# Two fused attention-and-FFN layers on one core: PSUM banks of phase A, one staged weight, reloads and low parts put in other places

## The chip, the cores and the metric

The kernel runs on one core of a Trainium2 chip. Its engines work side by side: TensorE (PE) multiplies matrices into eight PSUM banks, VectorE (DVE), ScalarE (ACT) and GpSimd (POOL) do the elementwise work, and SyncE (SP) issues most of the DMAs. The metric is the device time of one execution in microseconds, the median over several runs. The times of the profile are microseconds from the start of the profiled span unless they are marked ns.

## The reference

Two layers, with the same weights in both, run over x of 2048 rows and 640 columns:

```python
x = x + A(layernorm(x), wqkv, wo)
x = x + B(layernorm(x), w1, b1, w2, b2)      # and both once more
# A, 32 heads of 20: phi(t) = where(t > 0, t + 1, exp(t)) + 1e-6
kv  = einsum("bhsd,bhse->bhde", phi(k), v);  z = einsum("bhsd->bhd", phi(k))
o   = einsum("bhqd,bhde->bhqe", phi(q), kv) / (einsum("bhqd,bhd->bhq", phi(q), z)[..., None] + 1e-6)
A   = o @ wo
# B: h = x @ w1 + b1 (640 -> 1728);  B = max(h, 0)**2 @ w2 + b2 (1728 -> 640)
```

All of it is in float32.

## The kernel before

**Split numbers.** Each float32 matrix is held as a high part (rounded to the fast matmul type) and a low part (the rest). A product is three matmuls: low of one by high of the other, the other way round, and high by high. The high part is made by ACT (a copy), the low part by DVE (a subtraction), so the low part is always the later one.

**Phase A** (`for t in range(NT)`) goes through 16 tiles of 128 rows. For each tile it multiplies the normalised, transposed x (`xT`) by the weights of k and q (`kq`, five chunks, 1280 KB each with both parts), makes phi from the PSUM result (ACT takes the exponential, DVE the rest), and adds to G = xᵀ·phi(k) in banks 3 to 7 (`g_part`) for the tile before. The last 128 columns of k go to GT (`gt_part`), once for each pair of tiles; DVE adds that PSUM result to `GT_` (L613). Banks 0, 1 and 2 (`XB`) are for the parts of k and q and for GT. Tiles named in `LATE` compute only k in the loop ("late" tiles); their q follows afterwards. In such a tile the first part goes to bank 0, the second to bank 1, GT to banks 2 and 0; the next tile's first part goes to bank 0 again. In layer 0 ACT also moves blocks for the transpose of x (L459, sixteen moves for a tile), and `Prep` cuts w1 and w2 into high and low parts between the tiles: `prep_step(t, i)` is called at four places of each tile and takes one staged piece at each of them (`low`, then `high`; the high part is an ACT copy of what a DMA has brought, L295).

**Between the phases** kv is made from G, multiplied into wo, and split (`m_split`, L1050 the high part, L1051 the low part) into the five chunks of M. `proj` multiplies the first four tiles by M, and DVE adds the result to x, normalises it (`b_x1`, L748, L363, L373) and splits it for FC1 (L121).

**Phase B** runs in four groups of four tiles (512 rows). FC1 has 14 steps (`fc1`, 15 matmuls of 512 columns for most), FC2 has 28 steps (`fc2_step`, 7 products of 4 units each, in the order `ORDER`). The weights come from DRAM: `Units` holds a ring of six buffers, refilled in the order of use each time one comes free (`load_ring`, L338). Unit 0 of each of the seven products is loaded once for each layer and stays in the "w" buffers. Those five buffers hold, at other times, the five chunks of `kq`. Everything else is hung on steps: `at(g, n, f)` runs f after step n of group g (steps from NF = 14 on are those of FC2). `single` prepares the tiles of the next group: x goes out to DRAM (`spread_out`, issued by POOL), comes back in another order (`spread_in`, four DMAs issued by SP, L410), DVE transposes it (`turn`, L420), and ACT and DVE split it. `ffn_events` splits the hidden values into units of a small arena (ACT L1229, DVE L1233). The rows of ones and zeros that carry b2 are written by POOL memsets (L1157, L1158 at the start, L1161, L1162 in `ones_row`). `side_last` runs in the last group of layer 0: it reloads `kq` for layer 1 (L201) and prepares layer 1's first three tiles.

Instructions run in program order on each engine; SP's DMAs are issued in program order as well, and one that must wait for its buffer holds up those behind it. A new tile of a pool takes a buffer whose last use lies earlier in the program.

Of the kernel before, what the change touches and what calls it, by code (L numbers as in the profile page):

```python
# [17 lines left out]
DC = D // P  # L18
# [47 lines left out]
def kernel(  # L66
# [25 lines left out]
    def bank(i, n=1):  # L92
        return PS[:, 512 * i : 512 * (i + n)]
# [57 lines left out]
    class FirstLoads:  # L151


        def __init__(self):
            self.todo = [(nm, c) for nm in ("k", "q") for c in range(DC)]
            self.pending = []

            self.halves = []
# [160 lines left out]
    class Units:  # L319


        def __init__(self):
            self.at = {}
            self.ring = list(uses)
            self.stay = [(m, 0) for m in ORDER]
            self.spare = []
            self.free = 0
# [21 lines left out]
                self.at[m, k] = u  # L349

        def used(self, g, nm, c):
            if nm == "w1" or c > 0:
                self.free += 1

        def get(self, g, nm, c):
            return self.at[(nm, c) if nm != "w1" and c == 0 else (g, nm, c)]

    sts = {}

# [135 lines left out]
    def proj(ps, aT, w, cs=range(DC)):  # L495

        for c in cs:
            for j in range(2):
                s = slice(j * HD, (j + 1) * HD)
                mm3(  # L500
                    ps[:, j * 512 : j * 512 + HD], aT[:, 0, c, :], aT[:, 1, c, :],
                    w[c][:, 0, s], w[c][:, 1, s], c == 0, c == DC - 1,
                )

    x2 = [dram.tile([P, D], F32, name=f"x2_{t}", tag=f"x2_{t}") for t in range(NT)]

# [25 lines left out]
    for layer in range(N_LAYERS):  # L532
# [151 lines left out]

        pq, xr, pT, yzp, yzx, xn = {}, {}, {}, {}, {}, {}
        dens, xTb = {}, {}
        wu = Units()

        def b_load_pq(t):
            if t < NT:  # L690
# [102 lines left out]
        def prep_step(t, i):  # L793
            if layer == 0 and t in PREP_AT:
                if i == 0:
                    prep.mix()
                    prep.load(PREP.get(t + 1, ""))
                prep.low()
                prep.high()
                if i % 2 == 0:  # L800
                    prep.store(2)

        late = LATE[layer]
        q_end = None
        for t in range(NT):
            first = t == 0 and layer == 0
            early = t == 0 and layer > 0
# [64 lines left out]
            is_late = t in late  # L872
            f, fq = Phi(rtile()), None if is_late else Phi(ftile("rq"))
            n0 = HD if is_late else 512
            ps = ps_first if layer == 0 and t == 1 else part(t, 0, n0, bank(XB[0]))
            gs(0 if is_late or t == 1 and layer == 0 else 2)
            move(t + 1)
            f.exp(0, ps)
# [9 lines left out]
                x_begin(t + 2)  # L888
            f.rest()
            gt = t % 2 == 0 and t > 0  # L890
            ps = part(t, n0, D if is_late else 1024, bank(XB[1]))
            x_low = []
            if t + 1 in yza:
                x_low.append(xT_split(t + 1, x_end(t + 1), True))
# [16 lines left out]
                out=xh[t][:, 1], in0=xt[t], in1=xh[t][:, 0].bitcast(F32), op=ALU.subtract  # L911
            )
            if gt and not is_late:
                gt_part(t // 2 - 1, 0, bank(XB[0]))
            gs(1)
            prep_step(t, 2)
            if is_late:
                gs(1)
                if gt:
                    gt_part(t // 2 - 1, 0, bank(XB[2]))  # L920
                gs(1)
                if gt:
                    gt_part(t // 2 - 1, 1, bank(XB[0]))
            else:
                ps = part(t, 1024, 2 * D, bank(XB[2]))
                gs(1)
            k_post(t, f.r, [lambda: a_stats(t + 3)])
            if gt and not is_late:
                gt_part(t // 2 - 1, 1, bank(XB[1]))
            prep_step(t, 3)  # L930
            gs(DC)
            if not is_late:

                def q_end(t=t, f=fq, ps=ps):
                    f.exp(1024 - D, ps)
                    f.rest()
                    nc.sync.dma_start(pqd[t], f.r)

            move(t + 2, AHEAD)
        if q_end:  # L940
            q_end()
# [212 lines left out]
        )  # L1154

        R = bp.tile([P, 2, 2, KH, HT], F32, name="R", tag="R", bufs=1)
        nc.gpsimd.memset(R[FL:, :, 1, KH - 1], 0.0)  # L1157
        nc.gpsimd.memset(R[FL : FL + 1, :, 1, KH - 1], 1.0)  # L1158

        def ones_row():  # L1160
            nc.gpsimd.memset(R[FL:, 0, 1, KH - 1], 0.0)  # L1161
            nc.gpsimd.memset(R[FL : FL + 1, 0, 1, KH - 1], 1.0)  # L1162

        x1_odd["tile"] = bp.tile([P, TG, D], F32, name="x1", tag="x1", bufs=1)
        arena = tmp.tile([P, SLOTS, 2, 2, HT], R32, tag="T", name="arena", bufs=2)
# [2 lines left out]
        def fc1(g, c):  # L1168
            ps = bank(c % 4)
            u = wu.get(g, "w1", c)  # L1170
            xhi, xlo = xTb[0][:, 0], xTb[0][:, 1]
            if c == 13:
                w = u.rearrange("p (d f) -> p d f", d=DC)
                seq = [(w, xlo), (w, xhi)]
            else:
                w, wl = (u[:, j * D : (j + 1) * D].rearrange("p (d f) -> p d f", d=DC) for j in range(2))
                seq = [(w, xlo), (wl, xhi), (w, xhi)]
            for d in range(DC):
                for i, (a, bb) in enumerate(seq):
                    nc.tensor.matmul(  # L1180
                        ps, a[:, d, :], bb[:, d, :],
                        start=d == 0 and i == 0, stop=d == DC - 1 and i == len(seq) - 1,
                    )
            wu.used(g, "w1", c)
            return ps

# [105 lines left out]
        def at(g, n, f):  # L1292
            events.setdefault((g, n), []).append(f)
# [19 lines left out]
        def single(g, i):  # L1313

            t, b = TG * (g + 1) + i, OUTS[i]

            def on(n, f):
                if n < 0 and g > 0:
                    at(g - 1, NF + N_STEPS + 2 * n, f)
                elif n >= NF:  # L1320
                    at(g, NF + int(2 * (n - NF)), f)
                else:
                    at(g, max(n, 0), f)

# [12 lines left out]
            def out():  # L1337
                yzp.pop(t)
                for j in range(2):
                    s = slice(j * HD, (j + 1) * HD)  # L1340
                    ps.append(bank(6 + j)[:, :HD])
                    for c in range(DC):
                        a = pT[t][:, :, c * P : (c + 1) * P]
                        mm3(ps[j], a[:, 0], a[:, 1], M[c][:, 0, s], M[c][:, 1, s], c == 0, c == DC - 1)
                pT.pop(t)

            def add():
                for j in range(2):
# [12 lines left out]

            def load():
                yzx[t] = spread_in(xd.pop(t))

            n = NF + (1, 5, 9, 13)[i]
            at(g, n, load)
            steps(lambda: x_split(t), (g, n + 4), (g, n + 5), (g, n + 6))

        def ffn_events(g):
            for k in range(PAIRS):  # L1370
                at(g, 6 + k, lambda k=k: u_hi(g, k))
                at(g, 7 + k, lambda k=k: u_lo(g, k))
            for k in range(3):
                at(g, 9 + 2 * k, lambda k=k: s_op(1, k))
            at(g, 11, lambda: u_hi(g, PAIRS))
            at(g, 12, lambda: u_lo(g, PAIRS))
            s = NF
            if g > 0:
                at(g, 1, ones_row)
            at(g, s, lambda: s_op(1, 3))  # L1380
            for n in range(PAIRS + 1, N_STEPS):
                at(g, s + n - 4, lambda n=n: u_hi(g, n))
                at(g, s + n - 3, lambda n=n: u_lo(g, n))
            for k in range(PAIRS):
# [25 lines left out]
        def side_last():  # L1410
# [1 line left out]
                return  # L1412
            g, s = NG - 1, NF
            at(g, 2, lambda: load_kq(0))
            for c, n in ((1, 5), (2, 13), (3, 21), (4, 25)):
                at(g, s + n, lambda c=c: load_kq(c))
            xs = {}

# [6 lines left out]
            for t in range(3):  # L1425
                at(g, 1 + t, lambda t=t: a_load(t, x2))
                at(g, 4 + t, lambda t=t: a_stats(t))
                at(g, 5 + t, lambda t=t: a_apply(t))
                at(g, 6 + t, lambda t=t: store(t))
                at(g, s + 2 + 3 * t, lambda t=t: load(t))  # L1430
            for t in range(2):
                at(g, s + 8 + 4 * t, lambda t=t: xT_split(t, turn(yz0[t], True)))

# [66 lines left out]
```

## Time and profile before

| | before |
|---|---|
| median of the runs | 1346.39 us |
| lowest run | 1344.09 us |
| the profiled execution's own time | 1345.85 us |
| its span in the profile | 1344.1 us |
| mean granted PE clock | 0.997 |
| HBM read and written | 241.51 MB and 65.54 MB |

The page gives for each engine how long it was busy in the span. The waits name, for each line, what ended the idle time ahead of its instructions. In a timeline each row has the start, the duration, the engine, the line, what is written and read, the count, and in brackets the idle time before it with its releaser. In a table of stretches the columns are, after the stretch: its length, the busy time of PE, of PE's weight loads, of DVE, ACT and POOL (each with its count), the granted clock of PE, the mean share of the 16 DMA engines, and GB/s.

### The profile page before, as it was taken

What the parts mean: (1) busy time and instruction counts of PE and PEld (TensorE: products, weight loads), DVE (VectorE), ACT (ScalarE), POOL (GpSimd) and SP (SyncE); (2) the same over time, 40 slices, a digit from 0 to 9 for tenths busy, and PEclk for the clock granted to TensorE, in tenths of its full rate; (3) what the DMA queues carried; (4) which work ended last, traced back from release to release, by engine and by line L of the source; (5) the groups of instructions that cost most, each with busy time, mean ns of one, the idle gap of its engine ahead of it and who ended that gap; (6) DMA issues with size and microseconds to landing.
All of it is one profiled execution on the core that took longest, in us unless ns stands there. A gap on an engine that the chain in (4) does not pass through costs nothing.

```text
span 1344.1 us, 20919 instructions
## 1 busy us (share of the span) xinstructions
PE 1323.4 (98%) x7525; PEld 1202.6 (89%) x7525; DVE 848.4 (63%) x1575; ACT 733.0 (55%) x1594; POOL 166.7 (12%) x259
## 2 busy tenths in 40 slices
PE   8999999999999999999999999999999999999999
PEld 7888898989989988998978889888899899889888
DVE  7888957756844854833746677576567558458045
ACT  4888957785375457334313233387743753754342
POOL 2324310121001001001012222101100010010000
PEclk9999999999999999999999999999999999999999
DMA  6798993489974985896954456454869649749756
GB/s 196 219 282 268 337 343 120 153 327 373 320 296 146 291 306 169 265 359 222 346 185 128 128 133 172 118 192 151 304 207 319 248 161 317 305 148 297 277 190 215
DMA packets 134607, 320.28 MB, mean 238 GB/s; under 512 B 16663, under 2 KB 61847, under 8 KB 133864
## 3 DMA queue, kind: packets, MB, share of 16 engines
q1 hardware_dynamic: 127272, 296.65, 65.0%
q0 software_dynamic: 7232, 22.29, 6.4%
q8 instruction: 60, 0.98, 0.3%
q14 instruction: 43, 0.35, 0.1%
HBM read 241.51 MB, written 65.54 MB: 228 GB/s over the span
## 4 chain that ended last, share of the span: by engine, by line
PE 81%; DVE 6%; DMA 5%; ACT 5%; issue 2%; POOL 0%; SPq 0%; DVEq 0%; ACTq 0%; POOLq 0%
PE PS L473 29%; PE PS L1180 28%; PE PS L1249 22%; DMA z<-xb 3%; ACT z L459 2%; PE PS L1022 1%; DMA u<-kept 1%; DMA kq<-kept_kq 1%; DVE bn L363 1%; ACT z L439 1%; DMA xb<-xt 1%; DVE xT L489 0%; PE PS L831 0%; DVE y L420 0%; PE PS L621 0%
## 5 line engine op out<-in xcount | busy, mean ns | idle before, releaser
L1180 PE MATMUL PS<-xTb,u 128*128 128x512 f32 x1640 | 376.8, 390 | 1.0 <-DVE xTb L121 1.0
L1180 PEld LDWEIGHTS PS<-xTb,u 128*128 128x128 f32 x1640 | 306.7, 188 | 64.1 <-DVE xTb L121 1.5
L473 PE MATMUL PS<-kq,xT 128*128 128x320 f32 (+2 forms) x1575 | 286.0, 335 | 7.4 <-DVE GT L613 3.8
L473 PEld LDWEIGHTS PS<-kq,xT 128*128 128x128 f32 x1575 | 251.4, 189 | 36.1 <-issue 4.9
L1249 PE MATMUL PS<-u,arena 128*128 128x320 f32 x1680 | 257.5, 310 | 3.8 <-DMA u<-kept 2.4
L1249 PEld LDWEIGHTS PS<-u,arena 128*128 128x128 f32 x1680 | 248.8, 188 | 5.7 <-DVE arena L1233 2.7
L1233 DVE TENSOR_TENSOR arena<-R,arena 128x512 fp32r<-128x512 f32 x224 | 136.7, 616 | 137.9 <-ACT arena L1229 137.4
L1229 ACT ACTIVATE arena<-R 128x512 fp32r<-128x512 f32 x224 | 125.1, 572 | 142.3 <-PE PS L1249 136.9
L439 ACT ACTIVATE z<-y 32x160 f32<-32x160 f32 x512 | 171.2, 334 | 50.7 <-DVE y L430 43.2
L1192 ACT ACTIVATE R<-PS,b1sb 128x512 f32<-128x512 f32 x104 | 71.5, 688 | 131.4 <-PE PS L1180 130.4
L473 PE MATMUL PS<-kh,xh 128*128 128x512 f32 x480 | 126.2, 397 | 2.8 <-DVE xT L489 2.4
L473 PE MATMUL PS<-uM,pTs 128*128 128x320 f32 x720 | 109.4, 309 | 0.0
L473 PEld LDWEIGHTS PS<-uM,pTs 128*128 128x128 f32 x720 | 107.4, 188 | 1.9
L1249 PE MATMUL PS<-uw,arena 128*128 128x320 f32 x672 | 107.8, 309 | 0.0
L473 PEld LDWEIGHTS PS<-kh,xh 128*128 128x128 f32 x480 | 88.3, 190 | 18.8 <-DVE xT L489 2.6
L367 POOL TENSOR_SCALAR rs<-mv 128x1 f32<-128x1 f32 x64 | 35.0, 547 | 540.0 <-DVE mv L365 540.0
L1249 PEld LDWEIGHTS PS<-uw,arena 128*128 128x128 f32 x672 | 101.0, 188 | 0.2
L1210 DVE TENSOR_TENSOR R<-R 128x512 f32<-128x512 f32 (+1 forms) x128 | 78.3, 616 | 27.7 <-ACT R L1193 27.7
L459 ACT ACTIVATE z<-y 32x160 f32<-32x160 f32 x272 | 90.9, 334 | 4.5 <-DVE y L430 1.4
L575 ACT ACTIVATE r<-PS 128x512 f32<-128x512 f32 (+1 forms) x64 | 27.7, 434 | 105.5 <-PE PS L473 103.4
L582 DVE TENSOR_SCALAR r<-r 128x512 f32<-128x512 f32 (+1 forms) x64 | 21.1, 329 | 76.2 <-ACT r L575 76.0
L1193 ACT ACTIVATE R<-R 128x512 f32<-128x512 f32 x104 | 65.8, 633 | 3.3
(131 smaller groups left out, 1244.2 us busy)
## 6 DMA issues: line engine op xcount, KB each, us to landing
u<-kept SPq DMA_DIRECT2D x112, 640.0 KB, 5.9
u<-kept_w SPq DMA_DIRECT2D x104, 640.0 KB, 5.0
u<-kept SPq DMA_DIRECT2D x56, 320.0 KB, 6.1
kept<-uprep SPq DMA_DIRECT2D x49, 320.0 KB, 5.5
z<-xb SPq DMA_DIRECT2D x160, 80.0 KB, 5.3
pqt<-pq SPq DMA_DIRECT2D x32, 320.0 KB, 4.6
acc<-r POOLq DMA_DIRECT2D x28, 320.0 KB, 4.1
uw<-kept SPq DMA_DIRECT2D x14, 640.0 KB, 9.1
```

Of the source, the lines that this page charges most:

```text
L367: nc.gpsimd.tensor_scalar(rs, mv[:, 1:2], LN_EPS, None, op0=ALU.add)
L439: nc.scalar.activation(zv[j * B32 : (j + 1) * B32, :, i, :], yv[i * B32 : (i + 1) * B32, :, j, :], AF.Copy)
L459: nc.scalar.activation(zv[j * B32 : (j + 1) * B32, :, i, :], yv[i * B32 : (i + 1) * B32, j], AF.Copy)
L473: nc.tensor.matmul(ps, a, b, start=first and i == 0, stop=last and i == 2)
L575: nc.scalar.activation(self.e[:, a:b], ps, AF.Exp)
L1180: nc.tensor.matmul(ps, a[:, d, :], bb[:, d, :], start=d == 0 and i == 0, stop=d == DC - 1 and i == len(seq) - 1,)
L1192: nc.scalar.activation(r, v, AF.Relu, bias=b1sb[:, c : c + 1])
L1193: nc.scalar.activation(r, r, AF.Square)
L1210: nc.vector.tensor_tensor(out=quad(*out, k), in0=quad(*x, k), in1=quad(*y, k), op=op)
L1229: nc.scalar.activation(u[:, 0], v, AF.Copy)
L1233: nc.vector.tensor_tensor(out=u[:, 1], in0=v, in1=u[:, 0].bitcast(F32), op=ALU.subtract)
L1249: nc.tensor.matmul(ps, x, y, start=opens and k == 0 and p == 0 and e == 0, stop=k == PAIRS - 1 and p == b - a - 1 and e == 2, skip_group_c ...
```

## The change

1. **Banks.** `XB` is copied into a list `xb`; after a late tile with a GT part the list is rotated by one, so that the next tile begins in the next bank.
2. **One staged weight.** In layer 0, and in the last group alone, unit 0 of the last product (4) no longer comes from the buffer where it stays: it is one more load of the ring, ahead of unit 1 of that product. Its buffer's last use is then in the group before.
3. **k/q reload and bounced tiles.** With that buffer, chunk 4 of `kq` is reloaded at FC1 step 4 of the last group, not at FC2 step 25. The three bounced tiles of layer 1 come back at FC1 steps 10 to 12, not at FC2 steps 2, 5 and 8. The bounced tiles of `single` come back at FC2 steps 0, 3, 7 and 11, not at 1, 5, 9 and 13.
4. **Low parts last.** `proj` takes, for each chunk, low·high, high·high and then high·low, each for both halves. The first FC1 step of group 0 takes all products with the high part of x first and those with its low part at the end.
5. **One high part later.** `prep_step` leaves out the `high` of its first place in tile 1; the pieces follow one place later.
6. **Rows of ones.** The memset of both halves at the start of phase B is gone; `ones_row` takes a half and runs for the first group after FC1 steps 12 and 13.

```diff
-        def __init__(self):
+        def __init__(self, short):
             self.at = {}
             self.ring = list(uses)
+            self.moved = (NG - 1, ORDER[-1], 0) if short else None
+            if short:
+                self.ring.insert(self.ring.index((NG - 1, ORDER[-1], 1)), self.moved)
...
         def used(self, g, nm, c):
-            if nm == "w1" or c > 0:
+            if nm == "w1" or c > 0 or (g, nm, c) == self.moved:
                 self.free += 1
         def get(self, g, nm, c):
-            return self.at[(nm, c) if nm != "w1" and c == 0 else (g, nm, c)]
+            at_ring = nm == "w1" or c > 0 or (g, nm, c) == self.moved
+            return self.at[(g, nm, c) if at_ring else (nm, c)]
...
         for c in cs:
-            for j in range(2):
-                s = slice(j * HD, (j + 1) * HD)
-                mm3(
-                    ps[:, j * 512 : j * 512 + HD], aT[:, 0, c, :], aT[:, 1, c, :],
-                    w[c][:, 0, s], w[c][:, 1, s], c == 0, c == DC - 1,
-                )
+            for k, l in ((1, 0), (0, 0), (0, 1)):
+                for j in range(2):
+                    nc.tensor.matmul(
+                        ps[:, j * 512 : j * 512 + HD], aT[:, k, c, :], w[c][:, l, j * HD : (j + 1) * HD],
+                        start=c == 0 and (k, l) == (1, 0), stop=c == DC - 1 and (k, l) == (0, 1),
+                    )
...
-        wu = Units()
+        wu = Units(layer < N_LAYERS - 1)
...
                 prep.low()
-                prep.high()
+                if (t, i) != (1, 0):
+                    prep.high()
...
+        xb = list(XB)
...
-            ps = ps_first if layer == 0 and t == 1 else part(t, 0, n0, bank(XB[0]))
+            ps = ps_first if layer == 0 and t == 1 else part(t, 0, n0, bank(xb[0]))
...
+            if gt and is_late:
+                xb.append(xb.pop(0))
             move(t + 2, AHEAD)
...
-        nc.gpsimd.memset(R[FL:, :, 1, KH - 1], 0.0)
-        nc.gpsimd.memset(R[FL : FL + 1, :, 1, KH - 1], 1.0)
-        def ones_row():
-            nc.gpsimd.memset(R[FL:, 0, 1, KH - 1], 0.0)
-            nc.gpsimd.memset(R[FL : FL + 1, 0, 1, KH - 1], 1.0)
+        def ones_row(h):
+            nc.gpsimd.memset(R[FL:, h, 1, KH - 1], 0.0)
+            nc.gpsimd.memset(R[FL : FL + 1, h, 1, KH - 1], 1.0)
...
-            for d in range(DC):
-                for i, (a, bb) in enumerate(seq):
-                    nc.tensor.matmul(
-                        ps, a[:, d, :], bb[:, d, :],
-                        start=d == 0 and i == 0, stop=d == DC - 1 and i == len(seq) - 1,
-                    )
+            order = [(d, i) for d in range(DC) for i in range(len(seq))]
+            if g == 0 and c == 0:
+                order = [(d, i) for d, i in order if i] + [(d, 0) for d in range(DC)]
+            for d, i in order:
+                a, bb = seq[i]
+                nc.tensor.matmul(
+                    ps, a[:, d, :], bb[:, d, :], start=(d, i) == order[0], stop=(d, i) == order[-1],
+                )
...
             n = NF + (1, 5, 9, 13)[i]
-            at(g, n, load)
+            at(g, NF + (0, 3, 7, 11)[i], load)
...
-            if g > 0:
-                at(g, 1, ones_row)
+            for h in range(2 if g == 0 else 1):
+                at(g, 12 + h if g == 0 else 1, lambda h=h: ones_row(h))
...
             at(g, 2, lambda: load_kq(0))
-            for c, n in ((1, 5), (2, 13), (3, 21), (4, 25)):
+            at(g, 4, lambda: load_kq(4))
+            for c, n in ((1, 5), (2, 13), (3, 21)):
                 at(g, s + n, lambda c=c: load_kq(c))
...
-                at(g, s + 2 + 3 * t, lambda t=t: load(t))
+                at(g, 10 + t, lambda t=t: load(t))
```

In the rest of the tile loop every `XB[...]` becomes `xb[...]`.

More of the change, by code (lines that the diff above doesn't have):

```diff
@@ L890 @@
             gt = t % 2 == 0 and t > 0
-            ps = part(t, n0, D if is_late else 1024, bank(XB[1]))
+            ps = part(t, n0, D if is_late else 1024, bank(xb[1]))
             x_low = []
@@ L913 @@
             if gt and not is_late:
-                gt_part(t // 2 - 1, 0, bank(XB[0]))
+                gt_part(t // 2 - 1, 0, bank(xb[0]))
             gs(1)
@@ L919 @@
                 if gt:
-                    gt_part(t // 2 - 1, 0, bank(XB[2]))
+                    gt_part(t // 2 - 1, 0, bank(xb[2]))
                 gs(1)
                 if gt:
-                    gt_part(t // 2 - 1, 1, bank(XB[0]))
+                    gt_part(t // 2 - 1, 1, bank(xb[0]))
             else:
-                ps = part(t, 1024, 2 * D, bank(XB[2]))
+                ps = part(t, 1024, 2 * D, bank(xb[2]))
                 gs(1)
@@ L928 @@
             if gt and not is_late:
-                gt_part(t // 2 - 1, 1, bank(XB[1]))
+                gt_part(t // 2 - 1, 1, bank(xb[1]))
             prep_step(t, 3)
```

## The prediction

> **What bounds the kernel now.** First the page: the span, and each engine's share.
>
> ```profile
> span 1344.1 us, 20919 instructions
> PE 1323.4 (98%) x7525; PEld 1202.6 (89%) x7525; DVE 848.4 (63%) x1575; ACT 733.0 (55%) x1594; POOL 166.7 (12%) x259
> ```
>
> PE sets the time: it is idle for only 1344.1 - 1323.4 = 20.7 us, and no matmul is removed or added. Whatever the change gives must come out of these 20.7 us, or out of matmuls that run slowly; 2% of the time is 27 us. So the second view is that of PE's waits.
>
> ```profile
> PE PS L473 <- DVE GT L613: 3.8, 2, 2.6
> PE PS L473 <- DMA kq<-kept_kq: 2.8, 1, 2.8
> PE PS L1249 <- DMA u<-kept: 2.4, 1, 2.4
> PE PS L473 <- DVE xT L489: 2.4, 1, 2.4
> ...
> PE PS L1249 <- DVE arena L1233: 1.4, 3, 0.6
> PE PS L1180 <- DVE xTb L121: 1.0, 2, 0.5
> PE PS L473 <- DVE rl L583: 0.8, 2, 0.4
> PE PS L473 <- DVE uM L1051: 0.7, 2, 0.4
> PE PS L473 <- DVE kh L777: 0.4, 1, 0.4
> ```
>
> The columns after the colon are us in total, times, and the longest. The nine rows make 15.7 us. The pace of an undisturbed PE comes from a long piece of the chain that ended last:
>
> ```profile
> 327.00 43.22 PE PS L1249 x294
> ```
>
> That is 0.147 us for a matmul of 320 columns. An FC2 step is 43.22/28 = 1.54 us. I now take the stalls in turn and ask what is late next.
>
> **First tile of layer 0 (part 5 of the change).** Timelines of PE, ACT and DVE, and a stretch of the clock:
>
> ```profile
> 30.37 4.61 PE L473 MATMUL PS<-kh,xh 128*128 128x512 f32 x12 [2.39 <-DVE xT L489]
> 34.82 3.59 PE L473 MATMUL PS<-kq,xT 128*128 128x512 f32 x15
> 38.25 1.52 PE L473 MATMUL PS<-kh,xh 128*128 128x512 f32 x6
> ...
> 28.13 0.74 ACT L295 ACTIVATE uprep<-st 128x640 fp32r<-128x640 f32 x1 [3.83 <-DMA st<-in_B_w_dram]
> ...
> 29.49 0.82 DVE L489 TENSOR_TENSOR xT<-PS,xT 128x640 fp32r<-128x640 f32 x1 [2.22 <-ACT xT L486]
> 36.75 0.77 DVE L777 TENSOR_TENSOR kh<-r,kh 128x640 fp32r<-128x640 f32 x1
> ...
> 32.00:34.00 2.00, 2.00 (x6) 1.54 (x5) 1.86 (x6) 0.50 (x1) 0.20 (x1) 0.50 0.89 198
> ```
>
> ACT stands 3.83 us before a weight that is still on its way (L295); the copy of xT queued behind it is late, so is DVE's low part, and PE waits 2.39 us for the bank. Then it runs at half clock: the granted clock is 0.50, and twelve matmuls take 34.82 - 30.37 = 4.45 us, where (38.25 - 34.82)/15 = 0.229 us each would make 2.75; that is 1.7 more. Without this `high`, xT's copy goes ahead, DVE begins its low part where its idle time began (29.49 - 2.22 = 27.27) and ends at 28.1. PE would be ready at 30.37 - 2.39 = 27.98, so 0.1 stays. It comes to the next `g_part` at 28.1 + 2.75 + 3.43 = 34.3, not at 38.25. But that one needs kh, whose low part ended at 37.52, that is 7.2 us after xT's (30.31); one weight split of about 0.7 moves out of that stretch, so kh is ready at 28.1 + 6.5 = 34.6, or 0.2 later by the bank statistics between. I take 34.8: a gain of **3.4**, bounds 2.2 (the clock stays) and 4.1 (all). The skipped piece costs nothing: two are staged in this tile for four places.
>
> A wait of 2.8 us later on (kq) leaves the clock at 1.00, so the fall does not follow from a stall's length alone; here it lies right behind one:
>
> ```profile
> 681.00:684.00 3.00, 0.15 (x2) 0.14 (x2) 0.00 (x0) 0.00 (x0) 0.00 (x0) 1.00 0.80 287
> ```
>
> [...]
>
> **GT of tile 12 (part 1).** The same views later:
>
> ```profile
> 167.95 2.47 PE L473 MATMUL PS<-kq,xT 128*128 128x320 f32 x8 [2.64 <-DVE GT L613]
> 173.70 3.59 PE L473 MATMUL PS<-kh,xh 128*128 128x512 f32 x15
> ...
> 165.05 0.82 DVE L489 TENSOR_TENSOR xT<-z,xT 128x640 fp32r<-128x640 f32 x1
> 175.14 0.81 DVE L489 TENSOR_TENSOR xT<-z,xT 128x640 fp32r<-128x640 f32 x1
> ...
> 171.70 0.44 ACT L575 ACTIVATE r<-PS 128x320 f32<-128x320 f32 x1 [0.39 <-PE PS L473]
> 173.90 0.44 ACT L575 ACTIVATE r<-PS 128x320 f32<-128x320 f32 x1 [0.37 <-PE PS L473]
> ...
> 168.00:170.00 2.00, 2.00 (x8) 2.00 (x9) 1.49 (x4) 1.93 (x7) 0.98 (x2) 0.50 1.10 277
> ```
>
> With the next bank free, PE waits only for xT (165.87), and without the half clock its 30 matmuls (4.4) and 15 (3.4) end at 173.7, not at 173.70 + 3.43 = 177.1. But tile 14 then needs its own xT, which ended at 175.95; ACT is full there and waited for PE for only 0.39 + 0.37 us, so xT comes at best at 175.2. The gain is 177.1 - 175.2 = **1.9**, not 3.4; bounds 0 (another half clock behind the new wait of 1.5) and 3.9. In layer 1 the other GT stall has nothing behind it:
>
> ```profile
> 851.74 4.49 PE L473 MATMUL PS<-kq,xT 128*128 128x320 f32 x29 [1.12 <-DVE GT L613]
> ...
> 849.24 0.82 DVE L489 TENSOR_TENSOR xT<-y,xT 128x640 fp32r<-128x640 f32 x1
> ```
>
> PE is free at 850.6, xT is ready at 850.1: **1.1**. The rotation's other bank changes add no wait that I can find: a tile's second part now goes to a bank that GT has just left, but fifteen matmuls (2.2 us) stand ahead of it, and the q parts after tile 15 begin in bank 0, which that tile's second part holds, with five `g_part` of three matmuls (3.4 us) between. If DVE were later than that, each would cost what it is late.
>
> **Low parts (part 4) and rows of ones (part 6).**
>
> ```profile
> 232.18 0.82 DVE L1051 TENSOR_TENSOR uM<-Mr,uM 128x640 fp32r<-128x640 f32 x1
> ...
> 257.51 0.52 POOL L1157 MEMSET R<- 64x512 f32 x1
> ...
> 257.49 0.90 DVE L373 TENSOR_SCALAR xn<-x,mv,rs 128x640 f32<-128x640 f32 x1 [1.00 <-POOL rs L368]
> 918.05 0.61 DVE L373 TENSOR_SCALAR xn<-x,mv,rs 128x640 f32<-128x640 f32 x1 [1.00 <-POOL rs L368]
> ```
>
> M's low part ends at 233.0; four matmuls (0.59 us) now stand ahead of its use, more than the 0.36 waited: **0.7** for both layers. In FC1 ten matmuls (2.3 us) stand ahead of the low part of x, more than 0.5: 1.0. The normalisation beside the memset takes 0.90 us, the same form without one 0.61; the next operation on DVE falls in the memset too. With the memset gone the chain is at least 0.3 earlier, and 0.4 is all that the waits for rl hold: 0.8. Together **1.8**. The memsets that run later cost PE nothing: DVE is not on PE's path there.
>
> [...]
>
> **Bounced tiles and kq (parts 2 and 3).**
>
> ```profile
> 460.02 0.84 DVE L420 STREAM_TRANSPOSE y<-z 128x640 f32<-128x640 f32 x1 [1.85 <-DMA z<-xb]
> ...
> 648.05 5.88 SPq L410 DMA_DIRECT2D z<-xb  x4
> ...
> 668.09 0.55 SPq L201 DMA_DIRECT2D kq<-kept_kq  x1
> ...
> 673.91 9.91 DMA kq<-kept_kq
> ...
> u<-kept SPq DMA_DIRECT2D x112, 640.0 KB, 5.9
> ```
>
> DVE stands 1.85 us before a tile that is still being brought, and the arena behind it is late. Two steps earlier are 3.1 us, so the arena's 1.4 go: **1.4** (bound 0.7). In the last group SP spent 5.88 us on one such tile while a refill of the ring stood behind it; that is the wait of 2.4. The three tiles go to FC1, where SP passes them ahead of refills that are needed some twenty us later: **2.4** (bounds 0 and 2.4). Chunk 4 was issued at 673.91 and landed 9.91 us later; now chunk 3 is the last. It goes out after step 21, about 666, lands by 676 at that length, and is needed by the fourth chunk of a part that begins at 678.1 - 2.4 = 675.7, at 677.8: **2.8** (bounds 0 and 2.8). Its buffer is free, since the last use lies in the group before; were it not, SP would stand still in FC1 with all refills behind it. What the edit costs: one load of 640 KB, given out after step 17 and used at step 24, 10.8 us against the 5.9 of its row; 1280 KB and twelve small DMAs in FC1 of that group:
>
> ```profile
> 586.00:632.00 46.00, 46.00 (x205) 38.07 (x204) 9.82 (x20) 19.58 (x31) 5.26 (x13) 1.00 0.81 292
> ```
>
> 292 GB/s there become about 342, an estimate from 2.3 MB in 46 us; the ring is six steps of 3.4 us ahead, which hides a short queue.
>
> **The sum**: 3.4 + 1.9 + 1.1 + 0.7 + 1.8 + 1.4 + 2.4 + 2.8 = 15.5 us. The profiled execution took 1345.85 us, so 1330.4; the median shown, 1346.39, is 0.5 above it: **1331**.
>
> **Rivals.**
>
> *The half clock stays* (0.08). The slow stretch at 30 us has another cause, or the new wait of 1.5 at tile 14 brings one of its own: the first term falls to 2.2 and the second to 0, so 3.1 are lost: 1334. [...]
>
> *Phase A of layer 0 is bound by ACT and DVE* (0.14). PE's lead is used up before tile 13, as the 0.76 us of ACT's idle time suggest, and its first two terms vanish: 10.2 left, 1336. Against it: ACT idles in earlier tiles.
>
> *The kq reload stays late* (0.13), the change not doing what it says: FC1's added bytes push the ring back, SP issues chunk 3 late, and 2.4 and 2.8 stay: 10.3 left, 1336. With both, 5.5 left: 1340.
>
> *SP's queue turns slower* (0.10). The bounced tiles now stand earlier in front of the ring's refills, in six FC2 passes. A refill is issued eight steps ahead, 12.3 us, and lands in 5.9: if a tile's four DMAs hold SP for more than 6.4 us, PE waits. The 5.88 above shows that it comes near. With two stalls of 2.4 in each of six passes, 29 us, the time is 1331 + 29 = 1360. Against it, the usual tile:
>
> ```profile
> 349.61 1.74 SPq L410 DMA_DIRECT2D z<-xb  x4
> ```
>
> *The forecast* has 0.55.
>
> **The numbers.** The low end has the first two terms at their upper bounds (4.1 and 3.9, 2.7 more) and a little for shifts: 1327. The high end takes in the three smaller rivals: 1341. The slower rival is left out. Faster by over 2% would need 27 us, more than all idle time and two slow stretches of at most 1.7 each: 0.01; slower by over 2% is the upper part of the last rival: 0.03; within 2%, about what a measurement of this kernel can tell from no change: 0.96.
>
> **What would show it.** PE's waits without rows for GT, for kq, for xTb and for uM; no granted clock of 0.50 behind 28 us; a new wait for xT at tile 14, of about 1.5 us; kh in tile 2 at about 34.8; no arena wait. The prediction is wrong if PE's idle time stays over 12 us, if a wait for u<-kept appears in several FC2 passes, or if matmuls in `proj` take longer than 0.147 us.

## The result, and the profile after

The changed kernel takes 1326.34 us (median of four runs, 1326.07 to 1327.06), the kernel before 1345.24 in the same comparison (median of four). One run of the kernel before took 2423.89 us, far from the other three (1342.72 to 1346.39); it is left out of the ratio, though not of that median, nor of the 1346.39 that the forecast started from. The ratio is 0.9866, with a 95% interval of 0.9847 to 0.9886: 1.3% faster, which is clear of no change and inside the 2% that were called none. The forecast of 1331 had the sign and most of the size; it was 4.7 us too slow. Of these, 3.3 us lie in the sum: the profiled executions are 18.8 us apart (1345.85 before, 1327.06 after), where 15.5 were summed up. The rest comes from the medians: the forecast set its base 0.5 above the profiled execution, and the changed kernel's median lies 0.7 below its own. The low end of the range, 1327, is 0.7 above the measured median; the ratio applied to the 1346.39 would be 1328.3.

The page of the changed kernel, its first two parts:

```profile
span 1325.3 us, 20933 instructions
...
PE 1317.7 (99%) x7525; PEld 1200.1 (91%) x7525; DVE 848.4 (64%) x1575; ACT 735.1 (55%) x1594; POOL 167.2 (13%) x263
```

PE is idle for 7.6 us, where it was 20.7. It is also busy for 5.7 us less with the same 7525 matmuls. About half of that is two stretches at half clock that are gone (1.6 and 1.3 us); the rest belongs to the stalls that are gone, because each of them costs more than its idle time (worked out below, at the order of `proj`). PE's waits in the changed kernel (us in total, times, longest):

```profile
PE PS L625 <- POOL ident masks.py:199: 1.4, 1, 1.4
PE PS L477 <- DVE xT L493: 1.4, 2, 1.2
PE PS L477 <- DVE kh L781: 0.9, 2, 0.5
PE PS L1189 <- ACT arena L1237: 0.3, 1, 0.3
```

The waits for GT, kq, u<-kept, the arena's DVE, xTb, rl and uM are gone from the list. One line is new; it names ACT, and the trace shows that it was a weight (below, at the first FC1 step). The timeline of PE, at the places that the prediction named:

```profile
27.77 3.01 PE L477 MATMUL PS<-kh,xh 128*128 128x512 f32 x12
...
34.67 1.67 PE L477 MATMUL PS<-kh,xh 128*128 128x512 f32 x6 [0.48 <-DVE kh L781]
...
162.52 4.52 PE L477 MATMUL PS<-kq,xT 128*128 128x320 f32 x29 [0.25 <-DVE xT L493]
...
171.79 4.52 PE L477 MATMUL PS<-kq,xT 128*128 128x320 f32 x29 [1.18 <-DVE xT L493]
...
305.95 6.99 PE L1189 MATMUL PS<-xTb,u 128*128 128x512 f32 x30
313.28 2.52 PE L1189 MATMUL PS<-xTb,u 128*128 128x512 f32 x10 [0.34 <-ACT arena L1237]
...
667.29 12.57 PE L477 MATMUL PS<-kq,xT 128*128 128x512 f32 x60
```

The first row is the one that stood at 30.37 with 4.61 us; it now takes 3.01 and follows without a wait. The second is tile 2's `g_part`, 34.67 where 38.25 was. The fourth is the new wait for xT at tile 14. The last one begins layer 1. Its 60 matmuls have no listed wait for kq, but they take 12.57 us, where the second trace of the changed kernel has

```profile
667.73 12.21 PE L477 MATMUL PS<-kq,xT 128*128 128x512 f32 x60
```

The 0.35 us are a wait for chunk 3 of `kq`, too short for the list: its reload lands at 669.53, and the tenth matmul, the first to need it, begins at 669.58, where the pace would have it at 669.35. So this term is there with nothing to spare. The granted clock, in the stretch that had 0.50 (the table of stretches: the clock is the third number from the end):

```profile
32.00:34.00 2.00, 2.00 (x10) 1.49 (x8) 1.97 (x6) 1.94 (x6) 0.00 (x0) 1.00 1.04 212
```

Since both kernels run the same stages in the same order, the lead can be read stage by stage, as the difference of PE's start times in the two timelines:

| PE reaches | before | after | lead |
|---|---|---|---|
| `g_part` of tile 2 | 38.25 | 34.67 | 3.58 |
| end of phase A, layer 0 | 199.20 | 193.58 | 5.62 |
| end of the first `proj` | 244.60 | 238.40 | 6.20 |
| FC1, group 0 | 262.57 | 255.01 | 7.56 |
| FC2, group 0 | 326.83 | 320.03 | 6.80 |
| FC2, group 1 | 434.21 | 427.29 | 6.92 |
| FC1, group 2 | 478.43 | 470.41 | 8.02 |
| phase A, layer 1 | 678.11 | 667.29 | 10.82 |
| its end | 864.04 | 849.02 | 15.02 |
| end of `proj`, layer 1 | 909.43 | 893.83 | 15.60 |
| FC1, group 0, layer 1 | 927.40 | 910.45 | 16.95 |
| FC2, group 0, layer 1 | 991.65 | 974.59 | 17.06 |
| FC1, group 1, layer 1 | 1036.35 | 1017.71 | 18.64 |
| last FC2 | 1297.47 | 1278.74 | 18.73 |

The lead grows where a stall was, stays in between, and falls in one place: in FC1 of group 0 of layer 0, from 7.56 to 6.80 (from 7.67 behind the first step, which gives another 0.1: a loss of 0.86).

### The profile page after: what moved, and what is told of

The parts are those of the page before. It is cut to its first block, busy times and chain, and to the rows that moved or that the text cites. A ratio compares the mean times of both kernels' runs of the same rounds, so it can differ in the third digit from the quotient of the medians.

```text
span 1325.3 us, 20933 instructions
## 1 busy us (share of the span) xinstructions
PE 1317.7 (99%) x7525; PEld 1200.1 (91%) x7525; DVE 848.4 (64%) x1575; ACT 735.1 (55%) x1594; POOL 167.2 (13%) x263
## 4 chain that ended last, share of the span: by engine, by line
PE 85%; DVE 5%; ACT 4%; DMA 3%; issue 1%; SPq 1%; POOL 0%; ACTq 0%; DVEq 0%; POOLq 0%
PE PS L477 30%; PE PS L1257 25%; PE PS L1189 25%; PE PS L504 2%; ACT z L443 1%; PE PS L1030 1%; PE PS L1043 1%; ACT z L463 1%; DMA kq<-kept_kq 1%; DMA pqt<-pq 1%; DVE bn L367 1%; DMA kept<-uprep 1%; DVE uprep L301 0%; PE PS L837 0%; DVE xT L493 0%
## 5 line engine op out<-in xcount | busy, mean ns | idle before, releaser
L1237 ACT ACTIVATE arena<-R 128x512 fp32r<-128x512 f32 x224 | 128.3, 575 | 177.0 <-PE PS L1257 168.0
L1200 ACT ACTIVATE R<-PS,b1sb 128x512 f32<-128x512 f32 x104 | 71.5, 687 | 131.2 <-PE PS L1189 130.3
L371 POOL TENSOR_SCALAR rs<-mv 128x1 f32<-128x1 f32 x64 | 34.8, 544 | 546.3 <-DVE mv L369 546.3
L1270 DVE TENSOR_TENSOR x<-PS,x 128x320 f32<-128x320 f32 x112 | 53.6, 484 | 22.6 <-PE PS L1257 22.6
```

Source lines behind the costliest of these rows:

```text
L371: nc.gpsimd.tensor_scalar(rs, mv[:, 1:2], LN_EPS, None, op0=ALU.add)
L1200: nc.scalar.activation(r, v, AF.Relu, bias=b1sb[:, c : c + 1])
L1237: nc.scalar.activation(u[:, 0], v, AF.Copy)
L1270: nc.vector.tensor_tensor(out=v, in0=ps, in1=v, op=ALU.add)
```

## The experiments

In the first eight one part of the change is undone; "cost" is how much later PE reaches a place than in the first trace of the changed kernel. That trace has the 0.35 us for chunk 3 in phase A of layer 1, which most of the others lack, so what is read off is the step at the stage concerned, not the sum at the end. Each of the eight ran once; in the order below they took 1329.49, 1329.00, 1327.47, 1327.76, 1326.40, 1330.44, 1331.94 and 1328.61 us.

**The high part of tile 1 (part 5 undone).**

```diff
-                if (t, i) != (1, 0):
-                    prep.high()
+                prep.high()
```

> The changed kernel with the high part of the first place of tile 1 back (part 5 undone). Theory: the stall of about 2.4 us at 28 to 30 us comes back with a granted clock of 0.50 behind it, the g_part of tile 2 begins about 3.6 us later than in the changed kernel (34.67), and the 3.6 are still there at the end of phase A of layer 0 and at the end of the kernel (span about 1328.9). Rival (ACT and DVE pace phase A): the lead is given back before tile 13, and at the end of phase A the difference is under 1.5 us.

Its timeline of PE:

```profile
30.36 4.60 PE L477 MATMUL PS<-kh,xh 128*128 128x512 f32 x12 [2.45 <-DVE xT L493]
```

and its clock in that stretch:

```profile
32.00:34.00 2.00, 2.00 (x6) 1.58 (x5) 1.86 (x6) 0.52 (x1) 0.21 (x1) 0.50 0.80 187
```

The stall is back, 2.45 where it was 2.39, and so is the half clock. The cost is 3.37 us at the end of phase A, 2.76 from FC2 of group 0 on. So ACT and DVE do not pace phase A of layer 0, and that rival falls. The 0.6 between the two is not this edit's: the changed kernel's first trace loses 0.85 in the steps of FC1 of group 0 behind the first, this one only 0.23 (see the first FC1 step).

**The banks (part 1 undone).**

```diff
-            if gt and is_late:
-                xb.append(xb.pop(0))
```

> The changed kernel without the rotation of the banks (part 1 undone). Theory: the waits for GT come back at tile 13 of layer 0 (2.4 us or so, with a slow clock behind it) and at tile 15 of layer 1 (1.1), the wait for xT at tile 14 goes; at the end of phase A of layer 0 the cost is about 2.0 us, in layer 1 about 1.3, in all 3.3. [...]

Its timeline of PE:

```profile
164.75 4.63 PE L477 MATMUL PS<-kq,xT 128*128 128x320 f32 x30 [2.61 <-DVE GT L617]
```

and its clock behind the stall:

```profile
166.00:168.00 2.00, 2.00 (x16) 2.00 (x15) 1.20 (x3) 1.93 (x7) 0.98 (x2) 1.00 1.05 284
```

The same stall, 2.61 where it was 2.64, but the thirty matmuls behind it take 4.63 us at full clock, where the same thirty took 5.91 in the kernel before. The cost in layer 0 is 1.6 us, not 2.0; in layer 1 0.4 more (0.8 with the 0.35 of that trace), where 1.3 was expected. So a stall of this length makes the clock fall in one execution and not in another; what decides it is worked out in the part on the prediction.

**The first FC1 step (half of part 4 undone).**

```diff
-            if g == 0 and c == 0:
-                order = [(d, i) for d, i in order if i] + [(d, 0) for d in range(DC)]
```

> The changed kernel with the old order of the first FC1 step (half of part 4 undone). Theory: FC1 of group 0 begins 0.7 us later in both layers; in layer 1 the 0.7 stays, in layer 0 it is gone by the start of FC2 of group 0 (ACT paces that stage, the changed kernel lost 0.86 us of its lead there). Rival (the 0.86 are lost to the moved memsets): the loss stays 0.8 and the 0.7 is kept in both layers.

PE's waits have the low part of x again, and the row that named ACT is gone:

```profile
PE PS L1187 <- DVE xTb L121: 1.0, 2, 0.5
```

FC1 begins 0.66 us later than before that step in both layers. In layer 0 the cost goes from 0.77 to 0.60 and 0.01 through FC1 of group 0; in layer 1 the step is not given back. That fits the theory's numbers, but not its cause. The matmul at which PE stops there (the 31st of the forty that begin at 305.95) waits for ACT to have emptied its bank, which L1200 has done at 311.99, and for a weight that SP brings (`u<-kept_w`, issued at 304.46). The trace has sixteen steps of that DMA's semaphore, from 310.82 on; the last of them, taken here as the landing, is at 313.14, and the matmul begins at 313.28. In ten traces of the changed kernel and its variants this matmul begins 0.13 or 0.14 us behind that landing; in this run the weight is there at 312.43, before PE comes to it at 313.38, and nothing is lost. ACT's L1237 only happens to end nearby: with the part on layer 1's first tiles undone (below) it runs from 312.62 to 313.23, and the matmul begins at 312.65, without waiting for its end. In that run the forty matmuls have no wait at all in the timeline:

```profile
305.79 9.40 PE L1189 MATMUL PS<-xTb,u 128*128 128x512 f32 x40
```

The first trace loses another 0.25 us earlier in the stage, behind a weight that lands at 297.93 (the matmul begins at 298.06). How late these weights are differs between executions of the same code: against the kernel before, the steps of FC1 behind the first lose 0.85 and 0.73 us in the two traces of the changed kernel. Of the runs whose edits do not touch this stage, those without the rotation and with chunk 4 late lose 0.89 and 0.80, and those with the high part, the bounced tiles and layer 1's first tiles undone 0.23, 0.22 and 0.13. So what this half of part 4 gives in layer 0 was lost in the first trace, by weights that landed late; with the bounced tiles and with layer 1's first tiles undone PE comes to FC2 0.5 and 0.6 us ahead of this run.

**The rows of ones (part 6 undone).**

```diff
+        nc.gpsimd.memset(R[FL:, :, 1, KH - 1], 0.0)
+        nc.gpsimd.memset(R[FL : FL + 1, :, 1, KH - 1], 1.0)
...
-            for h in range(2 if g == 0 else 1):
-                at(g, 12 + h if g == 0 else 1, lambda h=h: ones_row(h))
+            if g > 0:
+                at(g, 1, lambda: ones_row(0))
```

> The changed kernel with the rows of ones written at the start of phase B (part 6 undone). Theory: the normalisation beside the memset takes 0.9 us again, the wait for rl of 0.4 is back in both layers and costs 0.6 each with the drain of the matmul ahead of it, 1.2 in all. Rival (the memsets at steps 12 and 13 cost the 0.86 us of FC1 group 0 in layer 0): that loss goes, and the kernel is about as fast as the changed one.

One of its waits of PE:

```profile
PE PS L477 <- DVE rl L587: 0.8, 2, 0.4
```

The normalisation beside the memset takes 0.90 us again (0.61 in the changed kernel, at 251.29, without one), as the theory has it. The step is 0.70 us in each layer, against 0.6 expected; in layer 0 the cost falls by 0.55 in FC1, because this execution loses only 0.31 there. By itself that would fit the rival too, since the loss is smaller without the moved memsets. But in the changed kernel they run from 315.12 on, behind the matmul at 313.28 that waits, so they are not what costs the lead there.

**The bounced tiles of `single` (part 3, first half undone).**

```diff
-            at(g, NF + (0, 3, 7, 11)[i], load)
+            at(g, n, load)
```

> The changed kernel with the bounced tiles of single loaded at FC2 steps 1, 5, 9 and 13 again. Theory: DVE waits for z again (0.7 to 2.4 us a tile), the arena's waits are back in FC2 of group 1 of layer 0 and of group 0 of layer 1, and cost 1.1 and 1.6 us, more than the 1.4 that PE's waits list, because each wait also costs the drain of the matmul ahead of it: 2.7 in all. Rival (the list is the whole cost): 1.4.

DVE's waits, one row each of the kernel before, of the changed one and of this one:

```profile
DVE y L420 <- DMA z<-xb: 29.0, 24, 2.4
```

```profile
DVE y L424 <- DMA z<-xb: 9.9, 11, 1.7
```

```profile
DVE y L424 <- DMA z<-xb: 25.2, 21, 2.1
```

DVE waits for z as it did before, and still PE has no wait for the arena; the cost is 0.2 us in FC2 of group 1 and nothing in layer 1. Neither theory had that. Either something else in the change clears the arena's waits, or they come and go: two more runs below.

**Layer 1's first tiles (part 3, second half undone).**

```diff
-                at(g, 10 + t, lambda t=t: load(t))
+                at(g, s + 2 + 3 * t, lambda t=t: load(t))
```

> The changed kernel with layer 1's first three tiles brought back at FC2 steps 2, 5 and 8 again, all of kq as changed. Theory: SP is held by a z load for over 4 us, a refill of the ring is late, and PE waits 2.4 us for u<-kept; 2.8 later at the end of FC2 of group 3. Rival (it was the kq reload at step 25 or the bytes, not the tiles): no wait for u<-kept, within 0.3 of the changed kernel.

Its timeline of PE:

```profile
648.20 4.41 PE L1257 MATMUL PS<-u,arena 128*128 128x320 f32 x18 [2.48 <-DMA u<-kept]
```

that of SP, where the tile is loaded:

```profile
639.54 5.67 SPq L414 DMA_DIRECT2D z<-xb  x4
```

and its clock behind the stall:

```profile
650.00:652.00 2.00, 2.00 (x10) 2.00 (x8) 2.00 (x5) 0.42 (x1) 0.00 (x0) 0.50 1.02 398
```

SP is held for 5.67 us by one tile, a refill is late, PE waits 2.48: as read from the profile of before. The cost is 4.25 us, not 2.8, because this time the clock fell (1.6 us of it).

**Chunk 4 of kq (part 3, with the freed buffer).**

```diff
-            at(g, 4, lambda: load_kq(4))
-            for c, n in ((1, 5), (2, 13), (3, 21)):
+            for c, n in ((1, 5), (2, 13), (3, 21), (4, 25)):
```

> The changed kernel with chunk 4 of kq reloaded at FC2 step 25 again (the staged weight stays in the ring). Theory: PE waits for kq at the start of layer 1, 2.5 to 3.0 us, all of it kept to the end. Rival (chunk 4 was late only because SP had been held before): a wait of under 1 us.

Its timeline of PE:

```profile
673.87 11.19 PE L477 MATMUL PS<-kq,xT 128*128 128x512 f32 x48 [3.04 <-DMA kq<-kept_kq]
```

and its clock behind the stall:

```profile
674.00:676.00 2.00, 2.00 (x5) 1.55 (x6) 0.00 (x0) 0.58 (x2) 0.00 (x0) 0.51 0.35 139
```

The wait is 3.04 with SP free, so it is the step and not SP that made it late. The cost is 4.3 us (4.7 without the 0.35 of the trace that it is compared with), again with a fallen clock, which in the first trace of before did not follow this stall.

**The order of `proj` (the other half of part 4).**

```diff
-            for k, l in ((1, 0), (0, 0), (0, 1)):
-                for j in range(2):
-                    nc.tensor.matmul(
-                        ps[:, j * 512 : j * 512 + HD], aT[:, k, c, :], w[c][:, l, j * HD : (j + 1) * HD],
-                        start=c == 0 and (k, l) == (1, 0), stop=c == DC - 1 and (k, l) == (0, 1),
-                    )
+            for j in range(2):
+                s = slice(j * HD, (j + 1) * HD)
+                mm3(
+                    ps[:, j * 512 : j * 512 + HD], aT[:, 0, c, :], aT[:, 1, c, :],
+                    w[c][:, 0, s], w[c][:, 1, s], c == 0, c == DC - 1,
+                )
```

> The changed kernel with the old order of proj (the other half of part 4 undone). Theory: the wait for uM of 0.36 is back in both layers and costs 0.58 each (0.36 and the drain, and small waits under the list's threshold): 1.2 in all. Rival (the new order is itself slower for a matmul): less than 0.7.

One of its waits of PE:

```profile
PE PS L477 <- DVE uM L1059: 0.7, 2, 0.4
```

The list has 0.36 for each, the stages say 0.59 and 0.60. The row of before shows where the rest is: twelve matmuls from 230.78 at 0.147 each would let the next begin at 232.54; it began at 233.06, 0.52 later, and 0.36 of that are listed. Idle time is counted from the modelled end of the last matmul, and that lies 0.31 us after its start and not 0.147: 0.16 us, called the drain here. And the first matmul behind the wait is slower: the next one begins 0.25 us after it, not 0.147. So each stall costs some 0.25 us more than its row says.

This run also waits 0.37 us for chunk 3 of `kq` at the start of layer 1 (0.7 us later in all than the runs that have no such wait): the reload lands at 670.53, just late.

**The kernel before, once more, and with one edit.**

```diff
-            at(g, n, load)
+            at(g, NF + (0, 3, 7, 11)[i], load)
```

(for the second of the two; the first has no edit)

> The kernel before once more, for its trace. Theory (the arena's waits of the first trace were late landings of that execution): the arena's waits of 1.4 us differ by more than 0.5 us or are gone, and the lead of the changed kernel in FC2 of group 1 of layer 0 (1.1) and of group 0 of layer 1 (1.6) shrinks with them; the stalls for GT, kq, u<-kept, xT, rl, uM and xTb stay within 0.3 us. Rival (the old steps of the bounced tiles make them, and some other part of the change clears them): the arena's waits are there again within 0.3 us.

> The kernel before with the bounced tiles of single loaded at FC2 steps 0, 3, 7 and 11 and nothing else changed. Both theories: no arena wait. If the arena's waits are in this one, the earlier load does nothing for them. DVE's waits for z fall from 29 us to about 10, as in the changed kernel.

The kernel before, second trace. From its waits:

```profile
PE PS L1249 <- ACT arena L1229: 3.4, 1, 3.4
...
PE PS L1249 <- DVE arena L1233: 2.1, 3, 1.5
...
DVE y L420 <- DMA z<-xb: 32.3, 26, 2.7
```

and its clock behind two stalls:

```profile
658.00:660.00 2.00, 1.98 (x7) 2.00 (x8) 2.00 (x5) 0.48 (x1) 0.00 (x0) 0.50 1.00 345
...
688.00:690.00 2.00, 2.00 (x7) 1.52 (x6) 1.27 (x3) 1.23 (x2) 0.00 (x0) 0.50 0.06 22
```

The arena's waits for DVE are 2.1 us, not 1.4, and in other places: in FC2 of group 1 of layer 0 this execution loses 1.1 less than the first one, in groups 0 and 1 of layer 1 0.7 and 0.9 more. (The row for ACT is the wait that was put down to u<-kept: it stands behind the same 12 matmuls of FC2 step 15, and SP was held 5.91 us ahead of it.) Both late stalls, of 3.38 and 2.23 us, are followed by half clock here; in the first trace neither was. It took 1351.58 us. The stalls for u<-kept and kq are 1.0 longer and 0.6 shorter than in the first trace, where 0.3 was expected.

With the tiles alone loaded earlier the kernel before takes 1342.01 us. Its DVE waits for z less, and no PE wait for the arena is left:

```profile
DVE y L420 <- DMA z<-xb: 9.5, 13, 2.1
```

Its lead over the first trace grows by 1.10 in FC2 of group 1 of layer 0 and by 1.60 in FC2 of group 0 of layer 1, the same 1.1 and 1.6 as in the changed kernel. None of the eleven traces with the earlier load has a wait of PE for the arena's DVE. So the earlier load does clear these waits; at the old steps they cost 2.7, 3.3 or 0.2 us in the three executions seen. What makes a z late enough in one and not in another is open.

**The changed kernel again, and with three more edits.**

```diff
-                prep.low()
+                if t == 1 and i > 1:
+                    prep.low(0 if i == 2 else 2)
+                else:
+                    prep.low()
...
+            if layer == 0 and t > 12:
+                for low in x_low:
+                    low()
+                x_low = []
             f.rest()
...
-            on(b - 4, lambda: blocks_move(yzp[t], (2, 3)))
+            on(b - 4, lambda: blocks_move(yzp[t], (2, 3), layer == 0 and g == 0 and i > 1))
```

(for the second of the two; the first has no edit. Where its third argument is true, `blocks_move` calls `nc.vector.tensor_copy` in place of ACT's copy.)

> The changed kernel once more, beside the next one: about 1326 us; the stages within 0.4 us of its first trace.

> The changed kernel with three edits at the waits that are left in layer 0: in tile 1 the low part of the first prepared piece is taken with the second, one place later, so that kh's low part is not behind it (gain 0.6: the wait of 0.48 and the drain); from tile 13 on the low part of xT is taken ahead of phi's rest (gain 0.6 of the 1.3 at tile 14, some of it lost at tile 15); in FC1 of group 0 DVE makes half of the block moves of tiles 6 and 7 in ACT's place (gain 0.8, the lead lost there, if ACT paces that stage). In all 2.0 us less than the changed kernel. If ACT does not pace FC1 of group 0, the last gain is absent: 1.2.

The changed kernel again: 1326.74 us, ratio to before 0.9869 (0.9852 to 0.9887); its stages lie up to 0.57 us from the first trace, where 0.4 was expected. With the three edits: 1326.64 us, 0.9869 (0.9851 to 0.9887): no difference that these runs can tell. The timeline of PE in the last one:

```profile
179.42 1.14 PE L479 MATMUL PS<-xh,kh 128*128 128x320 f32 x6 [0.84 <-DVE r L589]
...
306.13 9.45 PE L1198 MATMUL PS<-xTb,u 128*128 128x512 f32 x40
```

The waits of tile 2 and of tile 14 are gone, but later in tile 14 PE waits 0.84 for a bank that phi's rest now leaves later, and at the end of phase A only 0.1 of the 1.2 us is left. What the third edit does is not shown. The forty matmuls of FC1 before the last tile's product take 9.29 us from start to start, where the changed kernel took 9.68 and the pace asks for 9.09, and the row that named ACT is gone. But the run with layer 1's first tiles undone, which leaves ACT's block moves as they are, has 9.24: the weight lands earlier in both (312.91 and 312.52, against 313.14). A lost lead of 0.2 lies among the 0.13 to 0.23 of those three runs without this edit. That ACT paces the end of that stage is not borne out: the matmul begins 0.14 us behind the weight's landing here too.

## Why the prediction was right, and where not

**What bounds the kernel** was right: the 18.8 us are 13.1 of PE's idle time, 2.9 of half clock behind two stalls, and about 2.8 of the drains and slow first matmuls that go with stalls. What is left for PE to wait for are DVE in phase A of layer 0 (0.25 to 1.18 us) and, at two places, a weight that lands just in time or late.

**First tile of layer 0**: 3.4 forecast, 3.58 measured. In part this is luck of the trace that it was read from: 1.6 of it are the half clock, and the kernel before with the tiles loaded earlier has the same stall (2.45 us) without a fall. The step that names the next late thing holds too: `g_part` of tile 2 waits for kh. Rows of DVE in the changed kernel:

```profile
26.95 0.77 DVE L493 TENSOR_TENSOR xT<-PS,xT 128x640 fp32r<-128x640 f32 x1
...
33.85 0.77 DVE L781 TENSOR_TENSOR kh<-r,kh 128x640 fp32r<-128x640 f32 x1
...
170.92 0.81 DVE L493 TENSOR_TENSOR xT<-z,xT 128x640 fp32r<-128x640 f32 x1
```

kh ends at 34.62, forecast 34.6 to 34.8.

**GT of tile 12**: 1.9 forecast, 2.04 measured, with the wait for xT at tile 14 that limits it (1.18, where 1.5 was forecast; without a fall of the clock the same stall cost 1.6 in the run without the rotation): xT there ends at 171.73, 4.2 before its old 175.95, of which 3.6 are the first term. Taking the whole stall and its slow clock, 3.9, would have been wrong.

**Low parts and rows of ones**: 0.7 and 1.8 forecast; 0.58 + 0.60 and 1.36 + 1.35 measured. The terms were too small because they took the listed waits as the whole cost; there are two stalls in the first and four in the second, each with some 0.25 more. That the later memsets cost PE nothing held: they run from 315.12 us on, behind the place where the lead shrinks (the wait that ends at 313.28). What the prediction left out is whether the weights of FC1 in layer 0 come early enough for a PE that comes 7.6 us sooner: in the first trace two of them land late and take 0.86 back, in the other executions whose edits do not touch this stage 0.1 to 0.9. Why the same load lands sooner in one execution than in another was not tried.

**Bounced tiles and kq**: 1.4, 2.4, and 2.8 + 1.1 forecast; 2.68, 2.80 and 4.20 measured. The mechanisms were right, each shown by a run of its own; the first was mis-sized most. Two reasons: the 0.25 for each of the three stalls, and two stalls too short for the list. The kq term was right with a margin that wasn't there. The prediction gave chunk 3 11.8 us from its issue to its use (666 to 677.8); SP gives it out at 659.53, it is needed 9.8 us later and takes 10.0:

```profile
659.53 0.42 SPq L201 DMA_DIRECT2D kq<-kept_kq  x1
```

**The half clock** was the weakest step. I took the fall as belonging to the two stalls behind which it lay. The traces have sixteen stalls of 2.2 to 3.4 us, at the same four places; ten are followed by half clock and six are not, and length does not tell them apart: the wait for xT 2.39, 2.45 and 2.59 with and 2.45 without, for GT 2.64 twice with and 2.61 and 2.63 without, for u<-kept 2.32, 2.48 and 3.38 with and 2.41 without, for kq 2.23 and 3.04 with and 2.28 and 2.85 without.

What tells them apart in these traces is where a stall lies in time. The record of the granted clock has each fall last 3.41 us (3.413 for both in the first trace of the kernel before; one, in the second, lasts 6.83), and the falls of one execution begin whole multiples of 3.413 us apart: at 30.83 and 167.37 in that first trace (40 of them), at 32.14, 168.68, 656.78 and 687.50 in the second (40, 143 and 9). Lay that grid over each execution (in the one without a fall in it, from the fall behind its last instruction). Each of the ten stalls with a fall puts 2.05 to 3.04 us of idle time into one interval of its grid, and the fall begins where that interval ends; none of the six without puts more than 1.76 into any. The stall of 2.85 us for kq, for example, is cut by the boundary at 682.78 into 1.76 and 1.09. What made one fall last 6.83 us is not shown: only 1.24 us of idle time lie in the first interval that it covers. A fall cost 1.3 to 1.7 us, the long one 2.6. The grid lay differently in different executions of the same code (falls from 30.83 us on in one trace of the kernel before, from 32.14 in the other), and two of its four stalls were hit in the one, all four in the other; a stall of under 1.8 us was not hit in these traces.

**The rivals**: phase A bound by ACT and DVE and SP turning slower fell; no FC2 pass of the changed kernel waits for u<-kept. The kq reload staying late fell as it was priced: 0.35 us of wait are left in the first trace, none in the second. Half a clock staying did not occur in the changed kernel, which has no stall of 2 us left.

## What to carry to other kernels

When one engine is busy for 98% of the time, list its stalls, and for each ask what is late next; the answer was right here within 0.2 us for the first two stalls, where the next late thing was looked for, and wrong where it was not (0.86 us of the lead handed to FC1 of group 0, two of whose weights landed late, were lost there in the first trace). Count for each stall of PE its idle time and about 0.25 us more here, and for a stall over 2 us the chance of a half clock behind it (ten of the sixteen of 2.2 to 3.4 us here). When a wait names an engine whose result the waiting instruction does not read, look at what else it waits for; here it was a DMA, which landed 0.14 us ahead of the matmul. Before a small wait is explained, or an edit is said to clear it, look at a second trace of the same kernel: the arena's waits for DVE were 1.4 us in one trace of the kernel before and 2.1, in other places, in the other.

## What the runs showed of the hardware that was not expected

A stall of PE of 2.2 to 3.4 us was followed by half clock in some executions and not in others (ten of sixteen), at 1.3 to 1.7 us each and once 2.6. In these traces the ten put 2.05 to 3.04 us of idle time into one interval of a grid of 3.413 us, which is read from the falls themselves; the other six put at most 1.76. The kernel before has four such stalls and its times spread from 1340.8 to 1347.7 us in one comparison; the changed kernel has none and spreads over 1.1 us.

Four DMAs of 80 KB each, which SP issued in 1.73 to 3.02 us the other 39 times in the first trace of the kernel before, held it for 5.67 to 5.91 us in four executions, each time 5.5 to 6.3 us after a reload of 1280 KB had been issued (in the one whose landing the trace has, it was on its way from 633.82 to 643.81, and SP was held from 639.54 on); why the issue waits was not tried.
